# Batch 0's variances in four portions, pair transposes on other slots, and two constant fills on GpSimd, in a fused attention and MLP kernel

## The chip, the core and the metric

The kernel runs on one core of a Trainium2 chip. The metric is the device time of one execution, in microseconds. Slots, batches and heads are counted from 0. TensorE is called PE in the profile, VectorE DVE, ScalarE ACT, GpSimd POOL, and the queue that issues most transfers SP.

## The reference

Eight batches of eight heads go through causal attention with a bias that comes from a running sum. The heads of a batch are put side by side to 512 columns, normalised, and sent through a two-layer MLP with a residual.

```python
def _attn_ref(q, k, v, s):                      # q, k, v: 8 x 8 x 576 x 64; s: 8 x 8 x 576
    scores = scale * np.matmul(q, k.transpose(0, 1, 3, 2))
    cum = np.cumsum(np.maximum(s, 0.0), axis=-1)
    bias = -(cum[:, :, :, None] - cum[:, :, None, :])
    scores = np.where(causal, -1000000000.0, scores + np.minimum(bias, 0.0))
    scores = scores - np.max(scores, axis=-1, keepdims=True)
    attn = np.exp(scores)
    attn = attn / (np.sum(attn, axis=-1, keepdims=True) + 1e-09)
    return np.matmul(attn, v)

def _moe_ref(x, g_ln, w_ch1, w_ch2):            # x: 8 x 576 x 512
    mu = np.mean(x, axis=-1, keepdims=True)
    var = np.mean((x - mu) ** 2, axis=-1, keepdims=True)
    xn = (x - mu) / np.sqrt(var + 1e-06) * g_ln
    ch = np.maximum(xn @ w_ch1, 0.0) @ w_ch2    # 512 -> 2048 -> 512
    return x + ch
```

## The kernel before

The whole program is written out in one order by hand: every engine takes its instructions in the order in which the code emits them, and waits only for the data and the buffers of each.

**Batch 0** is worked in row tiles of 128 (`PLAN`, lines 870 to 880: a list of small steps). It ends with the scores of head 0 of batch 1 (`S8`), the last tile's scores and their exponential (`Sk`, L743, L750, and `xk`, L754).

**From then on** the loop of line 953 runs a slot `n` for each head of batches 1 to 7, n = 8 to 63. In a slot stand, in this order: what `pre(n)` issues (loads, casts, constants); the transposes of a pair of heads, where the table `PAIRS` has one (line 959); the scores of head n with their three exponentials (`scores`, L360, L371) and, from head 10 on, four causal selects on GpSimd (L379); one MLP unit of four matmuls whose relu goes to VectorE (L548; L829 for batch 0's early units of 16 small matmuls, L816); in even slots the last 64 rows of two heads (`scores_d`, L395, with the exponential L406 and the select L409); a second MLP unit, its relu on ScalarE (L550, L827); and, from slot 10 on, the product with v for head n-2 (`pv`, L436: 15 matmuls, and on VectorE L444, L446 and L453). From slot 16 on a few more MLP units end the slot. The second half of an MLP is L558, its output is put together on VectorE in L567, which needs the factor `rstd` of its batch.

**Pairs.** K and q of heads 8 to 19 (the rest of what `NPE` covers) come as two heads at a time, loaded by GpSimd's queue with a cast (L155). `qk_pair` transposes them on TensorE (L303: six matmuls for k, six for q) into two PSUM buffers of the pool `ps_t`, and copies them to `kq`: k by two copies on VectorE (L114), q by two on ScalarE (L112). Pair 5 holds the heads of slots 10 and 11, pair 6 those of 12 and 13, pair 7 of 14 and 15, pair 8 of 16 and 17, pair 9 of 18 and 19. The two buffers of `ps_t` are also used by `scores_d`, by the transposes of the normalised rows (L525) and by batch 0's products with v (`tile_pv`, L772, read on VectorE by `tile_norm`, L786 and L795).

**Batch 0's statistics.** The mean comes from sums (L496). The variance takes two `bn_stats` for each of four row tiles (`tile_stats`, L802), one `bn_aggr` for each (`ln_aggr`, L489), and then `rstd` (`ln_rstd`: L485 on VectorE, a power on GpSimd, L486). Batches from 1 on have their own in `pv_next` (`ln_stats`, L470, behind the product of every second head).

**Constant columns.** Heads from 20 on come as rows that GpSimd casts (L203) and to which it adds four bias columns out of the tile `cT` (L204). Two parts of `cT` are constants (L909, L910); the others are filled on VectorE by `bias_rows` in slot 9 (L285, L289).

**GpSimd's queue** early on issues the loads with a cast: batch 0's rows, v of batch 1, the weights in quarters (`ld_w1`, L225; `ld_w2`, L228) and the pairs. An issue waits until the eighth one before it has landed. Later GpSimd casts v of the coming batch (L116), does the selects and the row casts, in the order of the slots.

Of the kernel before, what the change touches and what calls it, by code (L numbers as in the profile page):

```python
# [19 lines left out]
def kernel(  # L20
# [11 lines left out]
    nc = tc.nc  # L32
    B, H, S, D = q.shape
# [5 lines left out]
    NF = S // P  # L39
# [61 lines left out]
    cT = const.tile([P, NT, 2, BH, 4], BF16, name="cT")  # L101
# [55 lines left out]
    def ld_cast_pair(g):  # L157
        ld_cast("k", g)
        ld_cast("q", g)

    def ld_v(b, t):
        if b >= B:
            return
        pn = P if t < NF else TL
        tmp = stage.tile([P, H, D], F32, name="vtmp", tag="st")
        nc.sync.dma_start(
            out=tmp[:pn], in_=v[b, :, t * P : t * P + pn, :].rearrange("h s d -> s h d")
        )
        loaded["v", b, t] = tmp


    def ld_cast_v(b, t):
        pn = P if t < NF else TL
        nc.gpsimd.dma_start(
            out=v_bf[b % 2][:pn, t, :, 0:D],
            in_=v[b, :, t * P : t * P + pn, :].rearrange("h s d -> s h d"),
        )

    def cast_v(b, t, eng):
        if b >= B:  # L180
            return
        pn = P if t < NF else TL
        copy_on(eng, v_bf[b % 2][:pn, t, :, 0:D], loaded.pop(("v", b, t))[:pn])


    def ld_rows(gam, t):
        pn = P if t < NF else TL
        b, h0 = gam // 2, (gam % 2) * G
        tmp = stage.tile([P, 2, G, D], F32, name="rowtmp", tag="st")
        for u, src in enumerate((k, q)):  # L190
            nc.sync.dma_start(
                out=tmp[0:pn, u],
                in_=src[b, h0 : h0 + G, t * P : t * P + pn, :].rearrange("h s d -> s h d"),
            )
        loaded["rows", gam, t] = tmp
# [3 lines left out]
    def cast_rows(gam, t):  # L199
        pn = P if t < NF else TL  # L200
        r = rows[turn[0] % NR]
        turn[0] += 1
        nc.gpsimd.tensor_copy(out=r[0:pn, :, :, 0:D], in_=loaded.pop(("rows", gam, t))[0:pn])  # L203
        nc.gpsimd.tensor_copy(  # L204
            out=r[0:pn, :, :, D:KA], in_=cT[0:pn, t, :, gam * G : (gam + 1) * G, :]
        )
        ready["rows", gam, t] = r

    def tr_rows(gam, t):
        pn = P if t < NF else TL  # L210
        r = ready.pop(("rows", gam, t))
        o = t * 2 * G * P
        nc.sync.dma_start_transpose(
            out=kq[home(gam)]
            .rearrange("p u h s -> p (u h s)")[:, o : o + 2 * G * pn]
            .rearrange("p (h s) -> p h s", s=pn),
            in_=r[0:pn].rearrange("p u h c -> p (u h c)"),
        )
# [4 lines left out]
    def ld_w1(c):  # L223
        sl = slice(c * 512, (c + 1) * 512)
        nc.gpsimd.dma_start(out=w1_bf[:, :, sl], in_=w1_r[:, :, sl])  # L225

    def ld_w2(i):
        nc.gpsimd.dma_start(  # L228
            out=w2_bf[:, 4 * i : 4 * i + 4, :], in_=w2_r[:, 4 * i : 4 * i + 4, :]
        )  # L230
# [3 lines left out]
    def aug(gam, eng, h0=0):  # L234
        r = slice(gam * G + h0, gam * G + G)
        i = home(gam)
        eng.dma_start(out=kq[i][D : D + 1, 1, h0:G, 0:S], in_=c_hi[r, :])
        for j in range(3):
            eng.dma_start(out=kq[i][D + 1 + j : D + 2 + j, 0, h0:G, 0:S], in_=c3[r, j, :])
# [83 lines left out]
    def qk_pair(g, k_engs, q_engs):  # L323
        tr_pair(g)
        evac_pair("k", g, k_engs)
        evac_pair("q", g, q_engs)
# [130 lines left out]
    def x_tiles(b):  # L457
        ts_ = [xb[b][:, t, :] for t in range(NF)]
        if b % 2 == 1:
            ts_.append(xm[b // 2])  # L460
        return ts_
# [20 lines left out]
    def ln_rstd(b):  # L482
        n = len(x_tiles(b))
        rs = rstd[:, b, 0:n]
        nc.vector.tensor_scalar_add(out=rs, in0=mvs[b][:, 0:n, 1], scalar1=1e-6)  # L485
        nc.gpsimd.tensor_tensor(out=rs, in0=rs, in1=mhalf[:, 0:n], op=ALU.pow)  # L486

    def ln_aggr(b, t):
        nc.vector.bn_aggr(out=mvs[b][:, t, :], in_=st[b][:, t, 0 : 2 if b == 0 else 3, :])  # L489
# [109 lines left out]
    def run_units(n, dve_first=False):  # L599
        for i in range(n):  # L600
            if queue:
                first_unit[0] = dve_first and i == 0
                queue.pop(0)()
# [64 lines left out]
    nc.gpsimd.memset(er[:, :, OD:EW], 0.0)  # L668
    ld_cast_pair(5)
    ld_w1(2)  # L670
    for t in range(NT):
        ld_cast_v(1, t)
    ld_w1(3)
# [108 lines left out]
    def tile_norm(t, g):  # L782
        pot = bank.pop(("V", t, g))
        pn = P if t < NF else TL
        rinv = small.tile([P, NT], F32, name="rinv", tag="rinv")
        nc.vector.reciprocal(out=rinv[0:pn, 0:G], in_=pot[0:pn, :, D])  # L786
        hs = slice(g * 256, (g + 1) * 256)
        x = xb[0][:, t, hs] if t < NF else xm[0][0:TL, hs]
        args = dict(
            out=x.rearrange("p (h d) -> p h d", d=D),  # L790
            in0=pot[0:pn, :, 0:D],
            in1=rinv[0:pn, 0:G].unsqueeze(2).to_broadcast([pn, G, D]),
        )
        if t == NF:
            nc.vector.tensor_tensor(op=ALU.mult, **args)  # L795
            return
        nc.vector.scalar_tensor_tensor(
            scalar=1.0, op0=ALU.mult, op1=ALU.mult, accum_out=sum0[:, t, g : g + 1], **args
        )

    def tile_stats(t, g):
        nc.vector.bn_stats(out=st[0][:, t, g, :], in_=xb[0][:, t, g * 256 : (g + 1) * 256])  # L802
# [98 lines left out]


    PAIR_LOADS = {11: 9}
    PAIRS = {9: 5, 11: 6, 13: 7, 14: 8, 15: 9}


    def pre(n):
        if n == 12:
            nc.vector.memset(cT[:, :, 0, :, 0], -1.0)  # L909
            nc.vector.memset(cT[:, :, 1, :, 1:4], 1.0)  # L910
        elif n == 14:
            for r in rows:
                nc.gpsimd.memset(r[:, :, :, KA:P], 0.0)
        if n in PAIR_LOADS:
            ld_cast_pair(PAIR_LOADS[n])
        if n in (11, 12):
            ld_w2(n - 9)
        if n in (8, 9):
            aug(n - 5, nc.sync)
        for gam in range(NPE, NG):  # L920
            m = n - 4 * gam
            if m == -6:
                ld_rows(gam, 0), ld_rows(gam, 1)
            elif m == -5:
                cast_rows(gam, 0), cast_rows(gam, 1)
                ld_rows(gam, 2), ld_rows(gam, 3)
            elif m == -4:
                tr_rows(gam, 0), tr_rows(gam, 1)
                cast_rows(gam, 2), cast_rows(gam, 3)
                ld_rows(gam, 4)  # L930
            elif m == -3:
                tr_rows(gam, 2), tr_rows(gam, 3)
                cast_rows(gam, 4)
                tr_rows(gam, 4)
        for nb in range(2, B):
            m = n - H * nb + (5 if nb == 2 else 7)
            if 0 <= m < NT:
                ld_v(nb, m)
            if 1 <= m <= NT:
                cast_v(nb, m - 1, "pool")  # L940
# [12 lines left out]
    for n in range(H, BH):  # L953
        b, h = n // H, n % H
        pre(n)

        end = next(m for m in (8 * i + 3 for i in range(2, B + 1)) if m >= n)
        nu = (2 if n < 16 else -(-len(queue) // (end - n + 1))) - 2
        if n in PAIRS:
            qk_pair(PAIRS[n], ("dve", "dve"), ("act", "act"))  # L960
        if n > H:
            scores(b, h)
        run_units(1, True)
        if h % 2 == 0:
            scores_d(b, h // 2)
        run_units(1)
        if n == H:
            for g in range(2):
                tile_pv(NF, g)
                tile_norm(NF, g)  # L970
            for t in range(NF):
                for g in range(2):
                    tile_stats(t, g)
        if n > 9:
            pv_next()
        if n == H + 1:
            bias_rows(trc)
        if n == H + 3:
            for t in range(NF):
                ln_aggr(0, t)  # L980
            ln_rstd(0)
        pend.append((b, h))
        lt = {2: (0, 1), 3: (2, 3, 4)}.get(h, ()) if b > 1 else ()
        for t in lt:
            ln_tr(b - 1, t, "act" if b == 2 else "dve")
            if t != 1 and t != 4:
                run_units(1)
                nu -= 1
        if n == 2 * H + 2:
            for t in range(3, NT):  # L990
                ln_xn(1, t)
        run_units(nu)
        if b > 1 and h == 3:
            run_units(len(queue))
            queue += batch_units(b - 1)
# [41 lines left out]
```

## Time and profile before

| | |
|---|---|
| median of 4 runs | 363.59 us (363.49 to 364.22) |
| the profiled execution's own time | 363.58 us |
| its span, first to last instruction | 361.9 us |
| mean granted clock of TensorE | 0.999 |

The profile is of one execution. "Busy" is the time in which an engine works on instructions; a wait is idle time in front of an instruction, put down to what ended it. Matmuls overlap, so the length of one is more than its share: their starts say more than their lengths.

| slot | scores start (us) | what else the slot had |
|---|---|---|
| 9 | 34.96 | pair 5 |
| 10 | 38.76 | |
| 11 | 42.32 | pair 6 |
| 12 | 45.16 | L909, L910 |
| 13 | 48.75 | pair 7 |
| 14 | 52.23 | pair 8 |
| 15 | 57.22 | pair 9 |
| 16 | 60.06 | |
| 17 | 64.88 | |
| 18 | 68.58 | |

The starts are those of each slot's first L360 on TensorE's timeline.

### The profile page before, as it was taken

How to read it: one execution, taken by the hardware profiler on the slowest of the kernel's cores; microseconds unless marked ns; L12 is line 12 of the kernel's file. 1: busy time of each engine (PE TensorE's matmuls, PEld its weight loads, DVE VectorE, ACT ScalarE, POOL GpSimd, SP SyncE). 2: the span in 40 equal slices, each digit the busy share in tenths (PEclk: the TensorE clock that was granted, in tenths of full speed). 3: DMA queues.
4: the chain of work that ended last, by engine and by line, in shares of the span. 5: the costliest groups of instructions: out<-in, count | busy, mean ns of one | idle time of the engine just before them, and what ended most of it. 6: DMA issues, size and time to landing. Idle time of an engine off the chain costs nothing.

```text
span 361.9 us, 8541 instructions
## 1 busy us (share of the span) xinstructions
PE 350.1 (97%) x3144; PEld 201.1 (56%) x3190; DVE 201.4 (56%) x545; ACT 185.3 (51%) x358; POOL 168.0 (46%) x449
## 2 busy tenths in 40 slices
PE   8998898999999999999999999999999999999995
PEld 3897655555555555555555555555555554444444
DVE  6886988774366535854384539544765492113111
ACT  4786897467633773167436743475347432501500
POOL 9994568475456564373776472646432110000000
PEclk9999999999999999999999999999999999999999
DMA  9999999999798998599889875989520011011003
GB/s 147 171 188 165 202 200 198 169 251 189 167 181 218 199 192 148 124 234 165 181 193 230 185 173 120 245 170 191 117 87 2 0 60 59 0 60 59 1 31 87
DMA packets 164202, 52.09 MB, mean 144 GB/s; under 512 B 152848, under 2 KB 159552, under 8 KB 164160
## 3 DMA queue, kind: packets, MB, share of 16 engines
q1 hardware_dynamic: 139248, 42.43, 55.4%
q0 software_dynamic: 23472, 8.33, 21.0%
q10 hardware_dynamic: 1440, 0.79, 0.9%
q8 instruction: 25, 0.41, 0.5%
q14 instruction: 17, 0.14, 0.1%
HBM read 37.11 MB, written 9.44 MB: 129 GB/s over the span
## 4 chain that ended last, share of the span: by engine, by line
PE 86%; DVE 8%; issue 2%; DMA 1%; ACT 1%; SPq 0%; ACTq 0%
PE ph L540 31%; PE py L558 31%; PE pot L436 6%; PE sa L360 3%; PE sc L360 3%; PE sb L360 3%; PE trx L525 2%; DVE xn L507 2%; PE st L714 1%; DMA tiletmp<-in_k_dram 1%; DVE kq L114 1%; PE ph L816 1%; PE trt L692 1%; DVE stats L470 1%; PE pot L772 1%
## 5 line engine op out<-in xcount | busy, mean ns | idle before, releaser
L558 PE MATMUL py<-w_bf,hT 128*128 128x512 bf16 (+1 forms) x570 | 133.8, 373 | 1.6 <-DVE yo L567 0.4
L540 PE MATMUL ph<-xT,w_bf 128*128 128x512 bf16 x457 | 112.5, 379 | 1.2
L550 ACT ACTIVATE hT<-ph 128x512 bf16<-128x512 f32 x100 | 59.7, 597 | 63.8 <-PE ph L540 63.8
L558 PEld LDWEIGHTS <-hT 128*128 128x128 bf16 x592 | 53.5, 98 | 49.0 <-issue 0.9
L540 PEld LDWEIGHTS <-w_bf 128*128 128x128 bf16 x544 | 48.6, 97 | 50.1 <-issue 2.9
L371 ACT ACTIVATE er<-sa 128x512 bf16<-128x512 f32 x56 | 33.4, 596 | 69.8 <-PE sa L360 37.6
L379 POOL TENSOR_SCALAR_AFFINE_SELECT er<-er 128x128 bf16<-128x128 bf16 x216 | 58.8, 297 | 17.6 <-ACT er L371 17.6
L548 DVE TENSOR_SCALAR hT<-ph 128x512 bf16<-128x512 f32 x36 | 24.9, 692 | 55.7 <-PE ph L540 50.6
L203 POOL CAST kq<-rowtmp 128x512 bf16<-128x512 f32 (+1 forms) x55 | 33.4, 607 | 40.2 <-DMA rowtmp<-in_q_dram 39.1
L360 PEld LDWEIGHTS <-kq 68*128 68x128 bf16 x412 | 29.7, 97 | 23.0 <-DVE kq L114 1.1
L436 PEld LDWEIGHTS <-er 128*128 128x128 bf16 x840 | 33.1, 98 | 13.3 <-issue 0.2
L567 DVE SCALAR_TENSOR_TENSOR yo<-py,rstd,xb 128x512 f32<-128x512 f32 x32 | 23.9, 748 | 25.4 <-PE py L558 17.2
L444 DVE RECIPROCAL rinv<-pot 128x5 f32<-128x5 f32 x56 | 10.8, 193 | 48.2 <-PE pot L436 47.9
L436 PE MATMUL pot<-v_bf,er 128*128 128x65 bf16 x840 | 34.7, 193 | 0.0
L371 ACT ACTIVATE er<-sc 128x512 bf16<-128x512 f32 x56 | 34.3, 612 | 0.0
L371 ACT ACTIVATE er<-sb 128x512 bf16<-128x512 f32 x56 | 33.5, 599 | 0.0
L116 POOL CAST v_bf<-vtmp 128x512 bf16<-128x512 f32 (+1 forms) x30 | 18.4, 612 | 31.2 <-DMA vtmp<-in_v_dram 30.0
L446 DVE TENSOR_TENSOR xb<-pot,rinv 128x256 f32<-128x256 f32 x56 | 23.8, 424 | 1.9
L486 POOL TENSOR_TENSOR rstd<-rstd,mhalf 128x4 f32<-128x4 f32 (+1 forms) x8 | 8.8, 1094 | 34.6 <-DVE rstd L485 28.2
L360 PE MATMUL sa<-kq 68*128 68x512 bf16 x56 | 21.4, 381 | 1.0 <-DVE kq L114 1.0
L470 DVE BATCH_NORM_STATS2 stats<-xb 128x6 f32<-128x128 f32 (+1 forms) x84 | 21.9, 320 | 0.4
L507 DVE SCALAR_TENSOR_TENSOR xn<-xb,mv,gb 128x512 bf16<-128x512 f32 x28 | 21.4, 763 | 1.0
(115 smaller groups left out, 369.9 us busy)
## 6 DMA issues: line engine op xcount, KB each, us to landing
out_dram<-yo SPq DMA_DIRECT2D x32, 256.0 KB
vtmp<-in_v_dram SPq DMA_DIRECT2D x24, 256.0 KB
rowtmp<-in_k_dram SPq DMA_DIRECT2D x44, 128.0 KB
rowtmp<-in_q_dram SPq DMA_DIRECT2D x44, 128.0 KB
w_bf<-in_moe_w_ch_dram POOLq DMA_DIRECT2D x8, 512.0 KB, 10.2
v_bf<-in_v_dram POOLq DMA_DIRECT2D x8, 128.0 KB, 6.9
kq<-kq SPq DMA_TRANSPOSE x55
kp<-in_k_dram POOLq DMA_DIRECT2D x6, 144.0 KB, 8.7
```

What stands on the lines that cost most here:

```text
L203: nc.gpsimd.tensor_copy(out=r[0:pn, :, :, 0:D], in_=loaded.pop(("rows", gam, t))[0:pn])
L360: nc.tensor.matmul(a[:, c + a0 - q0 : c + a1 - q0], lhsT=k_cols(b, h, kb), rhs=cols, start=True, stop=not (pe_mask and diag),)
L371: nc.scalar.activation(out=e[:, o : o + 512], in_=a, func=ACT.Exp, scale=scale)
L379: nc.gpsimd.affine_select(out=e[:, o : o + P], in_=e[:, o : o + P], compare_op=ALU.is_ge, fill=0.0, base=0, pattern=[[1, P]], channel_mult ...
L436: nc.tensor.matmul(pot[:, t, :], lhsT=e[:, o : o + P], rhs=vv[:, kb, h, :], start=(kb == 0), stop=(kb == last),)
L470: nc.vector.bn_stats(out=st[b][:, t, part, :], in_=x[:, lo:hi])
L507: nc.vector.scalar_tensor_tensor(out=xn, in0=tiles[t], scalar=mvs[b][:, t, 0:1] if b > 0 else mean0[:, t : t + 1], in1=gb, op0=ALU.subtrac ...
L540: nc.tensor.matmul(ph, lhsT=w1_bf[:, kd, fb * P : (fb + 1) * P], rhs=xT[:, kd, :], start=(kd == 0), stop=(kd == KD - 1),)
L548: nc.vector.tensor_scalar_max(out=hT[:, fb, :], in0=ph, scalar1=0.0)
L550: nc.scalar.activation(out=hT[:, fb, :], in_=ph, func=ACT.Relu)
L558: nc.tensor.matmul(py[t], lhsT=hT[:, fb, t * P : (t + 1) * P], rhs=w2_bf[:, fb, c0:c1], start=(fb == 0), stop=(fb == FB - 1),)
L567: nc.vector.scalar_tensor_tensor(out=yo, in0=py[t], scalar=rs, in1=x[:, c0:c1], op0=ALU.mult, op1=ALU.add)
```

## The change

Three things are changed.

- L802 and L489 of batch 0: before, all eight `bn_stats` stood in slot 8 and the four `bn_aggr` with L485 and L486 in slot 11. After, slots 9, 10, 11 and 12 take two `bn_stats` and one `bn_aggr` each, and slot 12 also L485 and L486.
- `PAIRS`: pair 5 moves from slot 9 to 8, pair 6 stays in 11, pair 7 stays in 13, pair 8 moves from 14 to 15, pair 9 from 15 to 17.
- The two constant fills of `cT` move from VectorE in slot 12 to GpSimd's queue before the loop, behind the issue of the third quarter of `w1` and in front of the five loads of v of batch 1.

```diff
     ld_cast_pair(5)
     ld_w1(2)
+    nc.gpsimd.memset(cT[:, :, 0, :, 0], -1.0)
+    nc.gpsimd.memset(cT[:, :, 1, :, 1:4], 1.0)
     for t in range(NT):
         ld_cast_v(1, t)
     ld_w1(3)
@@
-    PAIRS = {9: 5, 11: 6, 13: 7, 14: 8, 15: 9}
+    PAIRS = {8: 5, 11: 6, 13: 7, 15: 8, 17: 9}
 
     def pre(n):
-        if n == 12:
-            nc.vector.memset(cT[:, :, 0, :, 0], -1.0)
-            nc.vector.memset(cT[:, :, 1, :, 1:4], 1.0)
-        elif n == 14:
+        if n == 14:
             for r in rows:
                 nc.gpsimd.memset(r[:, :, :, KA:P], 0.0)
@@
             for g in range(2):
                 tile_pv(NF, g)
                 tile_norm(NF, g)
-            for t in range(NF):
-                for g in range(2):
-                    tile_stats(t, g)
         if n > 9:
             pv_next()
         if n == H + 1:
             bias_rows(trc)
-        if n == H + 3:
-            for t in range(NF):
-                ln_aggr(0, t)
-            ln_rstd(0)
+        if H < n <= H + 4:
+            for g in range(2):
+                tile_stats(n - H - 1, g)
+            ln_aggr(0, n - H - 1)
+            if n == H + 4:
+                ln_rstd(0)
```

## The prediction

> **What bounds the kernel now.** I read the page's first and fourth parts, then busy time by stretch, then the chain of waits from 28 to 72 us, then the timelines of TensorE, VectorE, ScalarE and GpSimd there.
>
> ```profile
> PE 350.1 (97%) x3144; PEld 201.1 (56%) x3190; DVE 201.4 (56%) x545; ACT 185.3 (51%) x358; POOL 168.0 (46%) x449
> ...
> PE 86%; DVE 8%; issue 2%; DMA 1%; ACT 1%; SPq 0%; ACTq 0%
> ```
>
> TensorE is busy for 97% of the span; 8% of the chain is VectorE's. The stretches (columns: window, length, then busy time and count for PE, PE's weight loads, DVE, ACT, POOL, granted clock, DMA share, GB/s) say where:
>
> ```profile
> 38.00:40.00 2.00, 1.24 (x16) 1.00 (x17) 1.97 (x3) 1.69 (x4) 0.52 (x2) 1.00 1.28 205
> ...
> 56.00:58.00 2.00, 1.36 (x18) 0.99 (x18) 1.92 (x5) 0.57 (x1) 0.28 (x2) 1.00 0.88 183
> ...
> 100.00:300.00 200.00, 197.93 (x1726) 110.73 (x1756) 116.50 (x321) 100.80 (x201) 97.60 (x292) 1.00 0.72 155
> ```
>
> From 100 us on TensorE lacks 1% of its time. It waits in the slots of batch 1, where VectorE is full. The chain there (start, length, what):
>
> ```profile
> 34.56 2.62 DVE stats L802 x8
> 37.18 0.71 DVE kq L114
> 37.90 0.81 DVE kq L114
> ...
> 38.76 0.39 PE sa L360
> ...
> 46.35 0.44 DVE mv L489 x4
> ...
> 47.82 0.86 DVE cT L910
> ...
> 55.31 0.80 DVE kq L114
> 56.12 0.81 DVE kq L114
> ...
> 56.97 0.41 PE trqk L303 x6
> ```
>
> In slot 9 the eight variances hold back VectorE's copies of pair 5, and the scores of slot 10 wait for those until 38.76; in slot 15 pair 9's q transposes wait until 56.97 for the copies of pair 8.
>
> **How I cost it.** Matmul work is the same before and after; what can change is how long TensorE stands. I lay the built order of TensorE, VectorE and ScalarE for slots 8 to 18 against rows of this trace, each instruction starting when its engine is free and what it waits for is there. The rows: a fused unit 0.89 (16 matmuls, 35.86 to 37.64 for two) or 0.865 (four matmuls), scores 0.66 (0.90 with masks), the 15 matmuls of L436 0.455, a pair's transposes 0.25 + 0.26; 0.20 from TensorE's last issue to its reader (45.16 to 45.36), 0.05 from a copy to TensorE (38.71 to 38.76). VectorE: a pair's k copies 1.64 (50.30 to 51.96), relu 0.61, L444 to L453 0.98 together (49.32 to 50.30), bias_rows 1.81 (39.34 to 41.15). ScalarE: q copies 1.62, an exponential 0.485. Laid against the kernel before, this gives score starts of 38.88, 45.18, 52.24, 60.05 and 64.85 in slots 10, 12, 14, 16 and 17; the trace has 38.76, 45.16, 52.23, 60.06, 64.88. TensorE's stalls in it: 0.28 + 0.36 (slot 9), 1.31 (10), 0.17 (12), 0.09 + 0.45 (14), 0.35 + 0.74 (15), 0.17 (16), 0.05 in bits: 3.97 us. That is all there is to win here.
>
> **Slot 8: pair 5 comes a slot earlier.** Its loads were issued at 20.37 and 21.00 and landed 5.6 and 5.7 later; TensorE reaches them at 30.61. The transposes take 0.51, the first unit 0.89, so TensorE is at L395 at 32.01. In the built program L395 takes the buffer that ScalarE's q copies free. ScalarE is in the batch-0 exponentials:
>
> ```profile
> 30.88 0.63 ACT L754 ACTIVATE er<-st 128x512 bf16<-128x512 f32 x1
> ...
> 35.16 1.62 ACT L112 COPY kq<-trqk 64x576 bf16<-64x576 bf16 x2 [1.84 <-PE trqk L303]
> ```
>
> The q copies can start at 31.36 and end at 32.98, so L395 starts at 33.03: a new stall of 1.02. Behind it on TensorE stand a unit, the 40 matmuls of L772 and the scores of slot 9, all later by it. In return slot 9 loses its 0.64 of stalls, and the copies are there long before slot 10 (37.95 instead of 38.76).
>
> **Slots 9 to 12: variances spread, constants gone.** Eight L802 took 2.61 together (34.49 to 37.10), four L489 0.46 (46.35 to 46.81). Now each of four slots has two variances and the aggregate that reads them. No row shows that sequence. From below, the grouped rates: 0.65 + 0.115 = 0.77. From above, each step run to its end with 0.05 between: 0.40 + 0.33 + 0.05 + 0.23 + 0.05 = 1.06, rounded up to 1.10. I take 0.98 (0.33 + 0.40, a 0.03 step, 0.22): the aggregate at 69.91 held its dependent L507 until 70.16, 0.25 against 0.115 in the group. VectorE then runs without a gap from 37.3 to 60.4: pair 6's k copies 43.21 to 44.85, so slot 12's scores start at 44.90, after a stall of 0.66 (0.26 earlier than before). L909 and L910 (0.33 + 0.86, and 0.39 of idle ahead of them) are gone from slot 12, but two variances, an aggregate and L485 (0.25) stand there: pair 7's k copies end at 51.85 and slot 14's scores start at 51.90, after 0.72.
>
> The Trainium skill, VectorE: DVE Perf Modes, section The DRAIN you can't avoid, has it that every VectorE instruction empties the pipe, and that chaining copies without semaphores between them saved nothing. By it the grouping would have been worth nothing and spreading would cost nothing (0.77 a slot), and the sum would be 361.7; the four aggregates in 0.46, each 0.22 long, speak against it, so the sum goes by 0.98.
>
> **Slots 14 to 17: pair 8 to 15, pair 9 to 17.** Slot 14 has no pair: its 0.54 of stalls go, but the 0.51 of transposes come later. Slot 15 has one buffer turn only, and its 1.09 goes. Pair 8's k copies stand on VectorE behind relu, L444 to L453 and the five L470 of slot 13 (1.75), end at 58.38, and slot 16's scores (58.43) wait 0.25 for them. Pair 9's copies lie at 63.97 to 65.61 on a VectorE that was idle for 1 us in 62 to 64, its q copies on a ScalarE idle for 2.99 before 65.35; slot 18 is ready at 68.15. The loads are there (q of pair 8 issued 35.97 and landed 9.5 later, q of pair 9 42.56 and 8.4). L485 one slot later, and L486 behind it on GpSimd (1.05, now behind slot 12's selects and ahead of slot 13's v cast, which waits for its load until 52.88 anyway), feed L567 only at 63.3: nothing.
>
> **GpSimd's constants.** Rows: its memsets of 128x480 in 0.45 and 64x520 in 0.53, so 320 + 960 elements about 1.25. From below 0.48 (two of the 0.24 of 128x32), from above 2.9 (the selects' 0.29 for 128). They stand in front of five v loads, w1's last quarter, pairs 6 to 8 and half of w2.
>
> ```profile
> 22.40 4.24 POOL L174 DMA_DIRECT2D v_bf<-in_v_dram  x5
> ...
> 29.51 0.64 POOL L155 DMA_DIRECT2D qp<-in_q_dram  x1 [1.47 <-DMA w_bf<-in_moe_w_ch_dram]
> ```
>
> GpSimd stands 1.47 at 29.5 for an earlier load, and again before each of the next six issues (0.20 to 1.01), so I cost them at nothing. Without that cover, q of pair 6 (issued 29.51, landed some 9.2 later, wanted at 41.1) would come 1:1 later beyond 2.4 us.
>
> **The sum.** Stalls after: 1.02 + 0.66 + 0.72 + 0.25 + 0.04 = 2.69, against 3.97: 1.28 less. The profiled execution took 363.58 (span 361.9), the median is 363.59: 362.3. With 0.77 a slot the same walk gains 1.88 (361.7); with 1.10, and the 0.39 of unexplained idle at 46.98 staying, 0.4 (363.2). That is the forecast's own range.
>
> **Rivals.** *No change, 363.5*: VectorE binds harder. Every 0.1 us more in each of the four slots costs 0.39; at 1.30 a slot the gain is gone. For it: VectorE has no gap for 23 us. Against: no row of the two lines reaches that.
> *More, 361.7*: the spread pieces at the group's rates, as above.
> *Slower, 365.1*: GpSimd's queue. It casts the next batch's v as loads land, and the selects of slot 14 stand behind the third:
>
> ```profile
> 57.96 0.61 POOL L116 CAST v_bf<-vtmp 128x512 bf16<-128x512 f32 x1 [1.72 <-DMA vtmp<-in_v_dram]
> 58.52 1.03 POOL L379 TENSOR_SCALAR_AFFINE_SELECT er<-er 128x128 bf16<-128x128 bf16 x4
> 59.52 0.29 POOL L409 TENSOR_SCALAR_AFFINE_SELECT er<-er 64x128 bf16<-64x128 bf16 x1
> ```
>
> L436 needs them, before at 62.66, now at 60.88: the cover is 1.07. The last quarter of w2 (issued 48.08, behind L486) now goes out near 45, ahead of that load. If its 512 KB at the 200 GB/s of this stretch go first, the load lands 2.6 later and 363.8 results; a whole period of these loads (52.88 to 57.96, 5.1) gives 366.3. It decides over the sign from 2.34 us late, and is slower than can be told from 3.1 (landing at 61.0). I price it at 3.9. Against it: those loads and the weights share queues that were never empty from 41 to 57.7, so an earlier issue moves no byte forward.
>
> **How the numbers follow.** Forecast 0.58, more 0.12, no change 0.17, slower 0.13. 0.2% (0.73 us) is about what a measurement of this kernel tells from none; a small part (0.03) of the forecast lies within it. Faster 0.67, same 0.20, slower 0.13. The range 361.6 to 363.6 leaves out the slower rival and little below; the likeliest alone has 361.7 to 363.2.
>
> **What would show it.** Right: no stall ahead of slot 10's scores; one of about 1 us ahead of L395 in slot 8, released by ScalarE; two of 0.5 to 0.9 ahead of the scores of slots 12 and 14, released by VectorE's copies; slot 18's scores 1.0 to 1.5 earlier than 68.58, and that lead kept to the end. Wrong: L436 in slots 16 to 24 waiting for L379; a lead that shrinks behind 70 us; stalls at L303 for loads.

## The result and the profile after

| | before | after |
|---|---|---|
| median | 363.51 us (62 runs) | 362.87 us (41 runs) |
| fastest and slowest | 363.22, 365.27 | 362.11, 366.93 |
| runs within 0.8 us of the fastest | 56 of 62 | 24 of 41 |
| the profiled execution, its span | 363.58, 361.9 | 362.34, 360.6 |

The ratio is 0.9985, with a 95% interval of 0.9977 to 0.9994. The gain between the medians is 0.64 us: half of the 1.28 forecast, real by its interval, and less than the 0.2% (0.73 us) that the prediction took as about what a measurement of this kernel tells from none. Profile against profile it is 1.24. The third row of the table is what has to be explained: the changed kernel's fastest executions are where the forecast has them, and many are not that fast.

The first and fourth parts of the changed kernel's page:

```profile
PE 349.3 (97%) x3144; PEld 201.1 (56%) x3190; DVE 201.6 (56%) x543; ACT 185.3 (51%) x358; POOL 170.3 (47%) x451
...
PE 85%; DVE 9%; ACT 2%; issue 2%; DMA 1%; SPq 0%; ACTq 0%
```

TensorE's work is the same. DVE has gone from 8% to 9% of the chain and ACT from 1% to 2%: the new waits are VectorE's copies and ScalarE's. TensorE's timeline of the changed kernel (start, length, engine, line, operation, tiles, shape; in brackets the idle time in front of it and what ended it):

```profile
32.79 0.19 PE L395 MATMUL sd<-kq 68*128 68x64 bf16 x1 [0.84 <-ACT kq L112]
...
37.69 0.38 PE L360 MATMUL sa<-kq 68*128 68x512 bf16 x1
...
44.52 0.39 PE L360 MATMUL sa<-kq 68*128 68x512 bf16 x1 [0.39 <-DVE kq L114]
...
51.62 0.39 PE L360 MATMUL sa<-kq 68*128 68x512 bf16 x1 [0.68 <-DVE kq L114]
...
58.23 0.39 PE L360 MATMUL sa<-kq 68*128 68x512 bf16 x1 [0.18 <-DVE kq L114]
...
67.08 0.38 PE L360 MATMUL sa<-kq 68*128 68x512 bf16 x1
```

These are the first matmul of L395 in slot 8 and the scores of slots 10, 12, 14, 16 and 18. Each forecast stall stands at its place, with the releaser forecast, and slot 10 has none. Slot 18 starts at 67.08 instead of 68.58, a lead of 1.50; 0.24 of it was there at slot 8 already (27.69 instead of 27.93), so the slots walked give 1.26. From 100 to 300 us TensorE is busy as it was (columns: window, length, busy time and count, granted clock, DMA share, GB/s):

```profile
100.00:300.00 200.00, 197.93 (x1722) 1.00 0.74 155
```

Between the two lies the part that I had not costed. The lead is 1.50 in each of slots 17 to 24 and 1.23 or 1.24 from slot 25 to the last. The product with v of slot 24 (L436), in the changed kernel:

```profile
96.54 0.88 PE L436 MATMUL pot<-v_bf,er 128*128 128x65 bf16 x15
```

and in the kernel before:

```profile
98.03 0.61 PE L436 MATMUL pot<-v_bf,er 128*128 128x65 bf16 x15
```

It starts 1.49 earlier and lasts 0.27 longer. It is the product of head 22, whose selects stand in slot 22. GpSimd's timeline of the changed kernel says what it waits for:

```profile
95.27 0.60 POOL L116 CAST v_bf<-vtmp 64x512 bf16<-64x512 f32 x1 [3.60 <-DMA vtmp<-in_v_dram]
95.83 1.03 POOL L379 TENSOR_SCALAR_AFFINE_SELECT er<-er 128x128 bf16<-128x128 bf16 x4
96.83 0.29 POOL L409 TENSOR_SCALAR_AFFINE_SELECT er<-er 64x128 bf16<-64x128 bf16 x1
```

The selects that L436 reads stand behind a cast of v that waits 3.60 for its load, and end at 97.12, when L436 is already under way. The same lines of the kernel before:

```profile
94.06 0.60 POOL L116 CAST v_bf<-vtmp 64x512 bf16<-64x512 f32 x1 [3.46 <-DMA vtmp<-in_v_dram]
94.61 1.03 POOL L379 TENSOR_SCALAR_AFFINE_SELECT er<-er 128x128 bf16<-128x128 bf16 x4
95.61 0.29 POOL L409 TENSOR_SCALAR_AFFINE_SELECT er<-er 64x128 bf16<-64x128 bf16 x1
```

There the selects are done at 95.90 and L436 starts at 98.03.

### The profile page after: what moved, and what is told of

It is laid out like the page before. It is cut to its first block, busy times and chain, and to the rows that moved or that the text cites. A ratio compares the mean times of both kernels' runs of the same rounds, so it can differ in the third digit from the quotient of the medians.

```text
span 360.6 us, 8537 instructions
## 1 busy us (share of the span) xinstructions
PE 349.3 (97%) x3144; PEld 201.1 (56%) x3190; DVE 201.6 (56%) x543; ACT 185.3 (51%) x358; POOL 170.3 (47%) x451
## 4 chain that ended last, share of the span: by engine, by line
PE 85%; DVE 9%; ACT 2%; issue 2%; DMA 1%; SPq 0%; ACTq 0%
PE py L558 31%; PE ph L540 31%; PE pot L436 6%; PE sa L360 3%; PE sc L360 3%; PE sb L360 3%; PE trx L525 2%; DVE xn L507 2%; PE st L716 1%; DVE kq L114 1%; DMA tiletmp<-in_k_dram 1%; PE trt L694 1%; PE pot L774 1%; PE ph L818 1%; ACT kq L112 1%
## 5 line engine op out<-in xcount | busy, mean ns | idle before, releaser
L379 POOL TENSOR_SCALAR_AFFINE_SELECT er<-er 128x128 bf16<-128x128 bf16 x216 | 58.8, 297 | 15.7 <-ACT er L371 15.7
L436 PEld LDWEIGHTS <-er 128*128 128x128 bf16 x840 | 33.2, 98 | 13.4
L436 PE MATMUL pot<-v_bf,er 128*128 128x65 bf16 x840 | 35.0, 193 | 0.0
L486 POOL TENSOR_TENSOR rstd<-rstd,mhalf 128x4 f32<-128x4 f32 (+1 forms) x8 | 8.7, 1091 | 32.7 <-DVE rstd L485 32.7
L507 DVE SCALAR_TENSOR_TENSOR xn<-xb,mv,gb 128x512 bf16<-128x512 f32 x28 | 22.3, 798 | 1.0
```

The costliest lines, as they stand in the source:

```text
L379: nc.gpsimd.affine_select(out=e[:, o : o + P], in_=e[:, o : o + P], compare_op=ALU.is_ge, fill=0.0, base=0, pattern=[[1, P]], channel_mult ...
L436: nc.tensor.matmul(pot[:, t, :], lhsT=e[:, o : o + P], rhs=vv[:, kb, h, :], start=(kb == 0), stop=(kb == last),)
L507: nc.vector.scalar_tensor_tensor(out=xn, in0=tiles[t], scalar=mvs[b][:, t, 0:1] if b > 0 else mean0[:, t : t + 1], in1=gb, op0=ALU.subtrac ...
```

## The experiments

The experiments form three sets, each on a chip of its own and with the kernel before beside it: 363.65 there (35 runs), 363.39 (22) and 363.40 (23). Above 363.9 are 14, 2 and 4 of these runs, so the scatter differs by set as well, and widths of scatter are best compared within one. The first set has the changed kernel again, the fills, the pairs and the casts of batch 2; the second the variances, the casts from batch 3 on and the version with grouped variances; the third the longer chain and the stores. The letters of the theories are explained in the expectations.

### Which part does what

*The changed kernel once more.*

> The changed kernel again, beside the next three on one chip. Its profile has TensorE at L436 of slot 16 at 60.68, 0.2 us after the selects of slot 14 end on GpSimd (60.51), and its runs scatter from 362.1 to 366.9 where those of the kernel before lie mostly within 0.4. Theory A (the landing of the third v load of batch 2 sets L436 of slot 16 in many executions): floor 362.1 to 362.4, median 362.7 to 363.1, scatter of 1 us and more upward. Theory B (the scatter is the chip's or the start's): the next kernels scatter alike. Theory C (the scatter comes from the loads of pair 6, which land 1.7 us ahead of their transposes): scatter here, and in every kernel with the fills on GpSimd.

363.37 (12 runs, 362.02 to 364.97), ratio 0.9984 [0.9968, 1.0001]. The profiled execution took 362.02 and kept its whole lead of 1.57 to the end: losing at slot 24 differs from execution to execution of one program.

*The fills back on VectorE, in slot 12.*

```diff
-    nc.gpsimd.memset(cT[:, :, 0, :, 0], -1.0)
-    nc.gpsimd.memset(cT[:, :, 1, :, 1:4], 1.0)
@@
+        if n == 12:
+            nc.vector.memset(cT[:, :, 0, :, 0], -1.0)
+            nc.vector.memset(cT[:, :, 1, :, 1:4], 1.0)
```

> The changed kernel with the two constant fills back on VectorE in slot 12. The walk of the prediction gives stalls of 0.84 in slot 13 and 1.56 ahead of slot 14's scores, in all 0.4 slower than the kernel before: 363.9. L436 of slot 16 comes at 62.5, 2 us behind the selects, so theory A wants little scatter, and so does C. If the fills' place does not matter on VectorE (the rival that the walk overrates VectorE), 362.3 to 362.9.

365.47 (363.89 to 367.0, 12 runs), ratio 1.0041 [1.0021, 1.0062]: slower than the kernel before. Slot 14's scores start at 53.37, 1.75 later than in the changed kernel; the walk gave 363.9 for an execution without losses further on, and the fastest has 363.89.

*Pairs alone* (the table `PAIRS` of the change; variances and fills as before).

> The kernel before with the new table of pairs alone: variances grouped in slot 8, fills on VectorE. The walk gives 1.3 us less than before, as much as the whole change (stalls 1.02 in slot 8, 0.84 in slot 10, 0.34 ahead of slot 14's scores, 0.25 ahead of slot 16's): 362.2, with the third v load landing near 57.9, 1 us of cover, hence less scatter than the changed kernel by theory A. A rival, that the spread variances are what makes the new table pay, gives 363.5 or more.

363.11 (362.14 to 365.25, 12 runs), ratio 0.9984 [0.9966, 1.0002]. The walk gave 362.2.

*Variances alone* (four portions; pairs and fills as before).

> The kernel before with the variances spread alone. The walk gives 1.35 us more than before (stalls of 0.84 in slot 13, 1.31 at pair 8's q transposes in slot 14): 364.9, floor 364.7. If the variances in slot 8 are what holds the kernel before, as its chain of waits shows them, 362.5 to 363.0.

365.05 (364.92 to 365.29, 5 runs), ratio 1.0043 [1.0031, 1.0056]. The walk gave 364.9.

So the new slots of the pairs carry the whole gain: the fastest executions show it (362.14 and 362.02 against 363.26 for the kernel before in that set), while the intervals of both medians just reach 1. Taking the variances apart costs 1.66 alone (365.05 against 363.39, the kernel before in that set) and 2.36 with the pairs moved and the fills on VectorE (365.47 against 363.11); the move of the fills buys back 2.10 (365.47 against 363.37). By the fastest executions the last two are 1.75 and 1.87.

The walk gives each kernel's fastest execution: 363.89, 362.14 and 364.92 against 363.9, 362.2 and 364.9, and 362.02 for the changed kernel against 362.3. Some of this agreement is luck: the walk starts from the profiled 363.58, some 0.3 above the fastest execution of the kernel before. From slot 8 to slot 18 the profiles have a gain of 1.26 for the changed kernel (1.28 by the walk), a gain of 1.27 for the pairs alone (1.3), a loss of 0.45 with the fills on VectorE (0.4) and of 1.64 for the variances alone (1.35). The medians lie above the fastest by about 1 us and more, but for the variances alone, whose five executions lie within 0.4 of each other. Theory C falls here: the pairs alone, with the fills on VectorE, scatter as widely as the changed kernel. So does the kernel with the fills back on VectorE, where theories A and C wanted little scatter. By the times alone theory B would stand; what follows goes by the places where executions lose.

### What takes the lead away

*The first idea: the casts of v of batch 2 ahead of the selects of slots 12 to 16.*

```diff
-            if 1 <= m <= NT:
+            if 1 <= m <= NT and nb > 2:
@@ behind scores_d
+        if 12 <= n <= 16:
+            cast_v(2, n - 12, "pool")
```

> The casts of batch 2's v stand on GpSimd behind each slot's selects and not in front. Theory A: L436 of slot 16 no longer depends on the v loads, so the upward scatter goes, and the median comes down to the floor, 362.1 to 362.4 (1.1 to 1.4 below the kernel before). Theories B and C: median and scatter as in the changed kernel, 362.7 to 363.1.

363.36 (362.11 to 364.84, 12 runs), ratio 0.998 [0.9962, 0.9998]: the median of the changed kernel. The idea fell, and its profile, of its slowest execution (364.84), shows why. TensorE's timeline:

```profile
83.36 1.10 PE L436 MATMUL pot<-v_bf,er 128*128 128x65 bf16 x15 [0.17 <-POOL er L379]
...
93.11 1.11 PE L436 MATMUL pot<-v_bf,er 128*128 128x65 bf16 x15
...
98.64 1.24 PE L436 MATMUL pot<-v_bf,er 128*128 128x65 bf16 x15 [0.25 <-POOL er L379]
```

Three products, in slots 21, 23 and 24, last 1.10 to 1.24 instead of 0.61 to 0.63; against the kernel before, these slots lose 0.80, 0.56 and 1.04. Its chain of waits (start, length, what):

```profile
88.44 3.71 DMA vtmp<-in_v_dram
...
92.20 0.61 POOL v_bf L116
...
93.75 3.94 DMA vtmp<-in_v_dram
...
97.74 0.61 POOL v_bf L116
...
98.35 0.25 POOL er L379
...
98.64 0.23 PE pot L436 x2
```

Read upwards: product, select, cast of v, its load, and further up another cast and its load. The place is slots 21 to 24, not slot 16.

*The casts of v behind the selects from batch 3 on*, four of five; in the changed kernel and in the kernel before.

```diff
-            if 1 <= m <= NT:
+            if 1 <= m <= NT and not (nb > 2 and m != 3):
@@ behind scores_d
+        if b > 1 and h in (2, 3, 5, 6):
+            cast_v(b + 1, h - 2, "pool")
```

> The changed kernel with four of the five v casts of each batch from 3 on behind the selects of their slot instead of ahead of them. Theory A2: the chain of SP's queue (v loads, row loads, transposes) is paced by the transfers and not moved by the change, and the selects of slots 19, 21 and 22 stand behind v casts that wait for it; the kernel before had 2.1 us of cover there (L436 of slot 24 at 98.03, selects done at 95.9), the changed one, 1.5 us ahead, 0.6 or less, so a late chain takes the gain back in slots 21 to 24. With the casts behind, no stall at L436 of slots 21, 23 and 24, and the scatter goes: floor 362.0 to 362.2, median 362.1 to 362.5. Theory B (the scatter lies elsewhere, or is the chip's): median 362.9 to 363.4 as in the changed kernel, and stalls elsewhere.

> The kernel before with the same four v casts behind the selects. By theory A2 its floor stays (363.3 to 363.5), as there was cover, and its occasional late executions (364 to 365.5, about a third on the last chip) go: median 363.4 to 363.6. By theory B they stay.

The changed kernel: 363.03 (362.07 to 363.69, 11 runs), ratio 0.9986 [0.9977, 0.9996]. The kernel before: 363.62 (363.24 to 364.98, 11), ratio 1.0006 [0.9996, 1.0017]. Both expectations of theory A2 were missed: the changed kernel's median is above the range given, and the late executions of the kernel before did not go (4 of 11 are above 363.9, against 2 of 22 without the edit). No L436 waits any more in the profile of the first (363.59), but its lead is 0.75 smaller at the start of slot 24, and 0.40 more at the start of slot 25. TensorE's timeline:

```profile
95.15 0.38 PE L360 MATMUL sa<-kq 68*128 68x512 bf16 x1 [0.59 <-DMA kq<-kq]
95.76 0.39 PE L360 MATMUL sb<-kq 68*128 68x64 bf16 x3 [0.23 <-DMA kq<-kq]
```

Now the scores of slot 24 wait, for the DMA transposes (L213) that put k and q of heads 24 to 27 into `kq`. The chain behind them:

```profile
75.89 0.67 DVE yo L567
...
76.56 0.54 SPq L585
...
79.19 5.00 DMA rowtmp<-in_q_dram
...
84.33 0.61 POOL kq L203
...
87.59 3.72 DMA vtmp<-in_v_dram
...
91.57 4.14 DMA kq<-kq
```

Loads of rows and of v, output stores of batch 0 and transposes stand in SP's one queue, in the order of the code. If that chain is late, TensorE meets it in slots 21 to 24, by the selects or by the scores. An obstacle taken from one of the two ways leaves the other. That would explain why the edit does so little; the late executions of the kernel before with it were not profiled.

*The chain made longer*, in both kernels: two more loads ahead of the rows of heads 24 to 27, into a tile that nobody reads.

```diff
     def ld_rows(gam, t):
@@
+        if gam == 6 and t == 0:
+            for j in range(2):
+                nc.sync.dma_start(out=extra[:, j], in_=k[b, h0 : h0 + G, 0:P, :].rearrange("h s d -> s h d"))
```

> The changed kernel with SP's chain made longer: two more loads of 256 KB each, into a tile that nobody reads, ahead of the first row load of heads 24 to 27 (slot 18). They cost SP about 1.1 us of issue and the queues 512 KB, some 2.5 us at 200 GB/s; no result changes. Theory A3: the lead is lost at slots 21 to 25 in nearly every execution and more than the lead: 363.7 to 365.0, that is 1 to 2 above the changed kernel. Rival B (the chain has room to spare): 362.8 to 363.4, no change.

> The kernel before with the same two extra loads. Theory A3: it reaches slots 21 to 25 about 1.3 us later than the changed kernel and so has that much more cover: it pays 1.0 to 1.5 us less for the same delay, 363.5 to 364.3, so that this and the changed kernel with the loads stand within 0.4 of each other and the change is worth next to nothing here. Rival B: 363.4 to 363.6, and the difference between the two stays at 0.6 or more.

The changed kernel: 363.58 (362.78 to 365.05, 12 runs), ratio 1.0007 [0.9992, 1.0022]. The kernel before: 363.55 (363.11 to 366.32, 12), ratio 1.0008 [0.9992, 1.0025]. The two are now alike: the change is worth nothing here, as the theory has it. The sizes are smaller than expected for the changed kernel (between theory A3, from 363.7, and rival B, up to 363.4), and at the lower end for the kernel before. The loads are smaller as well: the profile has them at 128 KB each, half of what the expectation counts. Not every execution pays: 4 of 12 of the changed kernel are at 362.78 to 362.89. The fastest executions tell it best: 362.78 against the 362.02 to 362.11 of the changed kernel without the loads, 363.11 against 363.20 of the kernel before. The same two loads cost the one some 0.7 and the other nothing; the changed kernel without the loads is from other sets, as this one has none. The two profiles are of later executions (364.85 and 364.21). In the changed kernel with the loads (lines from 191 on are 4 higher), on TensorE's timeline:

```profile
83.34 1.11 PE L440 MATMUL pot<-v_bf,er 128*128 128x65 bf16 x15 [0.42 <-POOL er L383]
...
93.36 1.11 PE L440 MATMUL pot<-v_bf,er 128*128 128x65 bf16 x15 [0.16 <-POOL er L383]
```

it loses 1.06, 0.82 and 0.93 in slots 21, 23 and 24. The kernel before with the loads loses nothing up to slot 23 and 0.99 in slot 24:

```profile
96.56 0.40 PE L364 MATMUL sb<-kq 68*128 68x64 bf16 x3 [0.81 <-DMA kq<-kq]
```

One mark can be set beside what each profiled execution loses: when SP issues the last load of v of the next batch (L166; with the loads, L167), 3.1 to 4.1 us ahead of its cast. How late that is for TensorE depends on its lead, so the table adds the two. The lead is that over the kernel before at the start of slot 21; the loss is what of it is gone at the start of slot 25. The two kernels with stores on ScalarE's queue (below) are left out, as they lose time before slot 21.

| kernel | last load of v issued | lead at slot 21 | sum | loss in slots 21 to 24 | the execution's time |
|---|---|---|---|---|---|
| variances alone | 91.27 | -1.35 | 89.92 | 0.00 | 364.92 |
| before | 90.97 | 0.00 | 90.97 | 0.00 | 363.58 |
| changed, again | 90.66 | 1.57 | 92.23 | 0.00 | 362.02 |
| before, casts behind | 92.41 | -0.13 | 92.28 | 0.00 | 363.72 |
| pairs alone | 91.08 | 1.46 | 92.54 | 0.00 | 362.14 |
| pairs, fills, casts behind (below) | 91.20 | 1.58 | 92.78 | 0.22 | 362.24 |
| fills back on VectorE | 93.16 | -0.26 | 92.90 | 0.24 | 364.12 |
| changed | 91.61 | 1.49 | 93.10 | 0.26 | 362.34 |
| before, chain longer | 93.02 | 0.21 | 93.23 | 0.98 | 364.21 |
| changed, casts behind | 92.84 | 1.18 | 94.02 | 1.15 | 363.59 |
| changed, casts of batch 2 behind | 93.75 | 1.16 | 94.91 | 2.40 | 364.84 |
| changed, chain longer | 93.81 | 1.43 | 95.24 | 2.81 | 364.85 |

The loss grows with the sum without an exception: nothing up to 92.54, about a quarter from 92.78 to 93.10, 1 to 2.8 us from 93.23 on. It does so across both kernels and both places of the casts. In all of these profiles the lead moves by no more than 0.03 from slot 26 to the last, which speaks against a scatter that shakes every part of an execution. Late loads come with either kernel; what differs is how much cover TensorE has when it gets there.

### Two that were to make it better

*Pairs and fills as changed, variances grouped as before, casts of v behind the selects.*

> New table of pairs and fills on GpSimd, the variances grouped as before, v casts behind. The walk of the prediction gives 1.6 us less than before against 1.3 for the whole change: the spread variances cost 0.3. So with A2 361.8 to 362.1, 0.2 to 0.4 under e8. If spreading the variances pays, it is slower than e8.

362.09 (361.9 to 362.71), ratio 0.9965 [0.9953, 0.9977]: the fastest version of the study, though of six runs. Its fastest execution is 0.1 to 0.2 below the changed kernel's. Up to slot 21 leaving the variances together is worth more: from slot 8 on this profile gains 1.64, that of the changed kernel 1.25, 0.39 apart, where the walk gave 0.3. Slot 24 takes back about as much from both (0.22 and 0.26). Why its six executions lie together, where 8 of 11 of its neighbour with spread variances are above 362.8, no run tells.

*Batch 0's output stores on ScalarE's queue*, to take them out of SP's chain; in the changed kernel and in the version above.

```diff
-                nc.sync.dma_start(out=out[b, t * P : (t + 1) * P, c0:c1], in_=yo)
+                (nc.scalar if b == 0 else nc.sync).dma_start(
+                    out=out[b, t * P : (t + 1) * P, c0:c1], in_=yo)
```

> The changed kernel with one edit: the four output stores of batch 0 are issued by ScalarE's queue, so SP's queue in slots 18 to 21 no longer waits for L567. Theory A3 (the walk gives the floor, 362.1; what the median has above it is SP's chain of v loads, row loads and DMA transposes, which the change doesn't move and which TensorE, now 1.5 us earlier, meets in slots 21 to 25): the chain gets back up to four waits and issues (0.5 to 0.9 each), so the executions draw together near the floor: median 362.1 to 362.6, and in the profile the lead over the kernel before at slot 26 is within 0.3 of that at slot 20. Rival B (the spread above the floor is nothing of that chain's, something that shakes every part of an execution): median 362.8 to 363.4 as in the changed kernel, and the same width of its executions (about 2.5 us between the first and the last but one). Rival C (ScalarE's own queue pays: its exponentials stand behind stores that wait for L567): 363.5 to 364.5, with stalls of TensorE released by ScalarE in slots 18 to 21.

> Pairs moved and fills on GpSimd, variances grouped as before, the v casts of batches from 3 on behind the selects, and batch 0's stores on ScalarE's queue: the candidate for a version below both kernels. The same without the stores' edit had 362.09. Theory A3: no loss at slot 24 any more (0.21 in that profile): 361.7 to 362.0. Rival B: 362.1, no change. Rival C: 363 or more.

369.14 (367.55 to 370.87, 5 runs), ratio 1.017 [1.015, 1.019], and 368.52 (367.32 to 368.75, 4), ratio 1.0127 [1.011, 1.0143]. Rival C, and the first is 4.6 above the top of its range. The chain of waits of the first:

```profile
76.34 4.17 DMA rowtmp<-in_q_dram
...
80.58 0.34 ACTq L585
...
80.96 0.59 ACT xT L112
...
81.60 0.38 PE ph L540
```

ScalarE's store goes out 0.07 after a load of SP's has landed (80.51), with which it shares no data; its `yo` was written by 78.68, 1.90 earlier. The store ahead of it had its `yo` at 72.07 and went out at 75.63. The profile puts ScalarE's idle time around the later store down to that load; that the stores wait for transfers of SP's queue is read from this and not tested. ScalarE stands 4.74 from 71.27 and 1.92 from 79.04, and TensorE waits 1.87, 0.98 and 1.46 for its copies to `xT`. The lead of 1.5 has become a lag of 3.76 by slot 21, and nothing is lost after that. So these two say nothing on SP's chain; a chain without the stores, in another way, wasn't tried.

## Why the prediction was right, and where it was half wrong

**The walk.** Forecast 1.28 of lead at slot 18, measured 1.26. Stalls forecast 1.02, 0.66, 0.72 and 0.25; shown as idle 0.84, 0.39, 0.68 and 0.18 (a matmul's modelled length hides part of each; the starts agree to 0.14 once the 0.24 of slot 8 is allowed for). As a forecast of an execution that loses nothing later, it held for the changed kernel and for the pairs alone, and was 0.3 short for the variances alone. One number of the text doesn't fit its own sum: slot 18 "ready at 68.15" would be a lead of 0.43, where 1.28 gives 67.30.

**The variances.** Taken at 0.98 a slot, between 0.77 and 1.10. Slot 10 of the changed kernel, on VectorE's timeline:

```profile
41.84 0.75 DVE L804 BATCH_NORM_STATS2 stats<-xb 128x6 f32<-128x256 f32 x2
42.63 0.21 DVE L489 BATCH_NORM_AGGREGATE mv<-stats 128x2 f32<-128x12 f32 x1
42.85 1.62 DVE L114 COPY kq<-trqk 64x576 bf16<-64x576 bf16 x2
```

From the first to the copy behind them it is 1.01, and in slots 9, 11 and 12 0.89, 1.02 and 1.03. By what the prediction made of the Trainium skill, VectorE: DVE Perf Modes, section The DRAIN you can't avoid, it would be 0.77 here: all four slots decide against that, and with it against the rival of 361.7. The section adds that an instruction that is not held starts earlier, which the prediction left out; in the group the four aggregates, 0.15 to 0.21 long each (the prediction reads 0.22), took 0.46 together.

**GpSimd's fills** cost TensorE nothing that its timeline shows (no L303 waits for a load), as said, and for the reason said. Its timeline:

```profile
22.57 0.86 POOL L671 MEMSET cT<- 128x320 bf16 x1
23.18 1.05 POOL L672 MEMSET cT<- 128x960 bf16 x1
24.14 4.24 POOL L174 DMA_DIRECT2D v_bf<-in_v_dram  x5
...
30.45 0.64 POOL L155 DMA_DIRECT2D qp<-in_q_dram  x1 [0.68 <-DMA w_bf<-in_moe_w_ch_dram]
```

They take 1.57 from 22.57 to 24.14 (1.25 estimated), and the wait in front of L155 shrinks from 1.47 to 0.68. What I didn't see is what they buy: back on VectorE, with the variances spread, they cost 1.75 by slot 14.

**The slower rival** was the right kind of thing at the wrong place. GpSimd's queue, a v cast that waits for its load, selects behind it, L436 behind those: that is what happens, in slots 21 to 24. In slot 16, where I priced it, the cover was said to be 1.07. It was about 0.2 in the profile: the third cast ran at 58.66, the selects ended at 60.51 and L436 began at 60.68. It held there, and the point from which it decides was wrong by 0.9.

**The step that failed** is the sum: 363.58 less the stalls of slots 8 to 18, with "that lead kept to the end". I had the page's 1% of idle from 100 us on, and read from it that nothing further on could take the lead back. I left out the slots between, 18 to 24, and the cover there, which is no idle time of TensorE's and so shows in none of its rows: before, the selects that L436 of slot 24 reads were done at 95.9, and L436 came at 98.03, 2.1 later. A lead of 1.5 leaves 0.6 of that, and in the changed kernel's profile the selects are 1.22 later than before, so it pays. The term left out is worth 0.64 between the medians, and 0.27 between the two profiles. The text named L436 waiting for L379 in slots 16 to 24 and a lead that shrinks behind 70 us as signs of being wrong; both are what the traces show. That the median still lies in the range is luck in part: its upper part was made for dearer variances and for no change, not for a loss behind slot 18.

That late loads cost an execution its lead is shown by the twelve profiles in the table, and the longer chain adds that delaying them on purpose does. That this accounts for the whole spread of the changed kernel is argued: of its 53 executions two were profiled, at 362.02 and 362.34. One spread is not accounted for. With the fills back on VectorE the lead is -0.26, so the cover is larger than in the kernel before, and its runs still go from 363.89 to 367.0; the profiled one (364.12) has its load as late as 93.16, and none of those above 364.5 was profiled.

## What to carry to other kernels

Where an engine is brought forward, ask of every queue that it meets later by how much that queue was early, and work this out as a list of covers (when the input was ready, when it was read), since idle time shows only the covers that are already gone. A gain above the smallest cover is given back there, and where transfers feed the queue it is given back in some executions and kept in others: compare the fastest runs with the walk and the median with the covers. A second way to the same late input makes a repair of the first worth little.

## What the runs showed of the hardware that was not expected

- The same load in SP's queue, the one of v at 56 us, took from 1.04 us to issue (the changed kernel again, 56.71) to 3.05 (casts of batch 2 behind, 56.38) in the profiled executions, with much the same program in front of it. Why is open.
- Output stores on ScalarE's queue went out 3.56 and 1.90 us after their data was there, the second of them 0.07 after a load of SP's queue had landed, and ScalarE's own work stood behind them, 4.74 and 1.92 us. Why they waited is not shown.
- A fill of 320 bf16 elements per partition, spread in steps, took GpSimd 0.86, and one of 960 took 1.05: far from in proportion to their elements.
